# Moving the query weights to ScalarE's queue, and a new order of all work, in an attention and GLU kernel

## The chip, the cores and the metric

The kernel runs on one core of one Trainium2 chip. The time is that of one execution on the device, in microseconds (us). The time before is the median of three runs; one of them was also profiled, and every time inside the kernel comes from that execution. In the profile the engines are called PE (TensorE), PEld (TensorE's weight loads), DVE (VectorE), ACT (ScalarE), POOL (GpSimd) and SP (SyncE). A q behind a name (SPq, ACTq) is the engine's queue, where it issues DMA transfers. Times are counted from the start of the span.

## What is computed

x is 2,048 tokens by 512, in bf16. Two branches read it, and a gate per token mixes them. A is attention with a memory: 32 heads of 16, in four segments of 512 tokens; each segment attends causally to itself, and reads a matrix M and a vector z that collect the keys and values of the segments before. B is a gated GLU with 1,792 inner features.

```python
g = sigmoid((x * gate_w).sum(-1, keepdims=True))
# A: q, k, v = x @ wq, x @ wk, x @ wv, split in heads; per segment s of 512:
a_dot = softmax(q_s @ k_s.T * Dh**-0.5 + causal) @ v_s
a_mem = (phi(q_s) @ M) / (phi(q_s) @ z + 1e-6)
o_s   = sigmoid(beta) * a_mem + (1 - sigmoid(beta)) * a_dot
M, z  = M + phi(k_s).T @ v_s, z + phi(k_s).sum()
a = concat(o_s) @ wo                       # phi(t) = t + 1 if t > 0 else exp(t)
# B:
b = (gelu(x @ w_gate) * (x @ w_up)) @ w_down
return g * a + (1 - g) * b
```

## The kernel before

All weights stay in SBUF once loaded. Tokens go through in four segments (0 to 3), and each segment has the same tasks, named by kind, segment and tile:

- `K`, `Q` (line 448; K of segment 0 is at 476, in three parts a, b, c): projections in four tiles of 128 features, each four matmuls of 512 columns that collect in one PSUM bank. `Kev`, `Qev` (441, 442) evict a bank with ScalarE (`:a`) or VectorE (`:d`). `kpada`, `kpadb` (487) spread the keys for the scores.
- `V` (498) in eight halves of 256 or 257 columns, `Vev` (505, 506). The 257th column is the gate's weight, which `gwtr` and `gwev` (768, 770) put there.
- `st` (601): a fill. Score matmuls of 32 rows, four at a time side by side, fill all four banks of one large PSUM tile (psX). `exp` (608) on ScalarE empties it in one instruction of 2,048 columns; `msk` (614) on GpSimd masks the diagonal. There is one psX, so the next fill waits for this exp. There are 72 fills.
- `pv` (643): probabilities times values, for two tiles at once; `tp`, `pvp`, `ota` (529, 666, 667, 672) on VectorE divide and transpose.
- `G`, `gelu`, `gd`, `U`, `h` (448, 697, 702, 719): the GLU's gate and up tiles, fourteen each; `out` (734) is the down projection, `wo` (748) attention's output projection, `wev` and `oev` (739, 742, 752) mix the two.
- `phk`, `phq` (460 to 464), `ktr`, `mz`, `nd`, `ndp`, `otr`, `otm`: the memory's phi, transposes and products. `vsh` (517) copies values to the other half of the partitions.

Dense results and pv share four PSUM banks; a task that opens a bank names it after a colon in the order (`G0_6:3`).

The order of all work is one list written out, `ORDER`. `schedule` (134) goes through it, takes for each task the engine that the list names, and gives each engine its instructions in the order of the list. Estimates such as `T_MM`, `issue` and `lat` in the tasks don't enter into the program. `plan` and `finalize` (171, 200) put a semaphore wait before each instruction for what it reads or overwrites. Each engine works through its own queue in order, so an instruction that waits holds all behind it, on SyncE and ScalarE their DMA issues too.

Loads are made by `load` and `ld_w` (324, 340). The last argument names another load that must have landed before this one is issued; `ld_x0_t2`, `ld_x0_t3` (361) and `ld_xt` (343) are DMA transposes of x, issued by SyncE. x of segment 0 comes in two ways: tokens 0 to 255 plainly (`x0_0` on SyncE, `x0_1` on ScalarE), turned by eight transposes on TensorE (`xtr0`, 785) and evicted by two copies of 512 columns (`xev0`, 794); tokens 256 to 511 by the two DMA transposes. Two loads of 256 KB bring wk, one on SyncE (blocks 2 and 3 of the contraction), one on ScalarE (blocks 0 and 1). K's part a needs blocks 2 and 3 of the first 256 tokens, part b blocks 0 and 1, part c all four of the last 256 tokens.

Before the data are there, TensorE multiplies ones by ones: `warm1` (45 matmuls of 80 columns) ahead of the transposes, and `warm2` (7 more) behind them (382).

SyncE issues in this order: x0_0, wk1, x0_t2, x0_t3, wq0, wq1, gw, beta, wv (once x0_t3 is there), wg0 (once wq1 is there), the four transposes of x's second segment, wu1, and so on. ScalarE issues x0_1 and wk0 ahead of everything else that it does.

Of the kernel before, what the change touches and what calls it, by code (L numbers as in the profile page):

```python
# [248 lines left out]
def _build(es, nc, A_x, A_wq, A_wk, A_wv, A_wo, A_beta, B_w_gate, B_w_up, B_w_down, gate_w, out):  # L249
# [90 lines left out]
    def ld_w(name, eng, dst, src, writes, size, wait=(), **kw):  # L340
        load(name, eng, lambda e: e.dma_start(dst, src), writes, size=size, wait=[("ld", w) for w in wait], **kw)  # L341
# [39 lines left out]
    for name, n, cols in (("warm1", 45, 80), ("warm2", 7, 80)):  # L381
        one(name, PE, 3.0, [I(lambda e, cols=cols: e.matmul(BK[s0.i][:, 0:cols], ones, ones[:, 0:cols], start=True, stop=True),
                              [], [bk(s0)]) for _ in range(n)], bias=9000.0, opens=name == "warm1")
# [400 lines left out]
    for p in (1, 0):  # L784
        one(f"xtr0_{p}", PE, 4 * T_TR, [I(lambda e, q=q, kb=kb, p=p: e.transpose(
            XB[:, 1024 * p + (kb % 2) * 256 + q * 128:1024 * p + (kb % 2) * 256 + q * 128 + 128],
            pt[stage[0]][:, q, kb * 128:(kb + 1) * 128], ident[:, :]),
            [("xs", 0, 0), ("xs", 0, 1), ("pt", stage[0]), ("ident",)], [("X", p)]) for kb in (2 * p, 2 * p + 1) for q in (0, 1)])
        dst = xT[0][:, 2 * p:2 * p + 2, 0:256]
        xin = XB[:, 1024 * p:1024 * p + 512].rearrange("p (k c) -> p k c", c=256)  # L790
        wr = [("xT", 0, kb, "h0") for kb in (2 * p, 2 * p + 1)]
        task(f"xev0_{p}", [
            (ACT, 0.477, [I(lambda e, dst=dst, xin=xin: e.activation(dst, xin, ACTF.Copy), [("X", p)], wr)]),
            (DVE, 0.335, [I(lambda e, dst=dst, xin=xin: e.tensor_copy(dst, xin), [("X", p)], wr)])], L_DVE)
# [72 lines left out]
exp0_0C Q0_2:0 G0_2:3 V0_2b:2 ld_x1_2 ld_x1_1 betab ld_x1_3 ld_x1_0 st0_0D Vev0_2b:a exp0_0D Gev0_2:d kpadb0_1
Qev0_2:d phka0_0 V1_2b:1 V0_0a:3 G1_6:2 V1_0b:0 Vev1_2b:d phka0_2 st0_0E Vev0_0a:d Vev1_0b:d G0_1:1 bexp Gev1_6:a
exp0_0E Gev0_1:d Q1_2:3 V1_3b:2 V1_3a:0 kpada0_3 Qev1_2:d Vev1_3a:d phkb0_2 phkc0_2 Vev1_3b:d st0_1A gz0 gqa exp0_1A
gr0 Q1_0:1 V1_0a:3 G1_5:0 Vev1_0a:d gqb Gev1_5:d st0_1B Q1_1:2 K1_0:3 exp0_1B phkb0_0 ld_wu1 ld_x2_0 G0_5:0 Qev1_0:d  # L870
kpadb0_3 vsh0_21 st0_1C exp0_1C Qev1_1:d ld_x2_1 ld_x2_3 ktr0_3 ld_wg1 Gev0_5:d V1_2a:1 K1_3:2 K1_1:0 vsh0_01
# [87 lines left out]
```

## Time and profile before

| | us |
|---|---|
| runs | 263.88, 264.18, 264.53 |
| median | 264.18 |
| the profiled execution | 264.53 |
| its span, first to last instruction | 262.8 |
| TensorE busy | 257.9 |
| ScalarE busy | 203.2 |
| VectorE busy | 197.4 |
| GpSimd busy | 99.1 |

The page says that 16.50 MB were moved, and that the granted clock of TensorE was 1.00 of full speed over the whole span. Matmuls overlap in the array, and each is shown from its start to its modelled end, so two neighbours overlap in the record: what a matmul costs is read from the distance of two starts. Busy time in the page is that of the engine having at least one instruction in work. In a line of the timeline stand the start, the length, the engine, the line of the code, the operation, what it writes and reads, its shape, and the count of instructions merged into it; in brackets the idle time ahead of it and what ended it.

### The profile page before, as it was taken

The page shows a single profiled execution, that of the slowest core. Times are in us where ns is not written, and L with a number is a line of the kernel's source. Part 1 is how long each engine was busy: PE and PEld are TensorE (multiplying, and loading weights), DVE is VectorE, ACT ScalarE, POOL GpSimd, SP SyncE. Part 2 cuts the span into 40 slices and gives each one's busy share as a digit, 9 for nine tenths or more (in the row PEclk, how much of TensorE's full clock was granted, in tenths as well). Part 3 has the DMA queues.
Part 4 walks back from the last instruction along what each step waited for, and adds up shares of the span by engine and source line. Part 5 has one row for each costly group of instructions (what it writes and reads, how often), then busy time and mean ns, then how long its engine had stood idle before and what let it go on. Part 6 is the DMA issues. An engine that isn't in the chain of part 4 may idle for free.

```text
span 262.8 us, 6704 instructions
## 1 busy us (share of the span) xinstructions
PE 257.9 (98%) x2849; PEld 122.5 (47%) x2849; DVE 197.4 (75%) x412; ACT 203.2 (77%) x171; POOL 99.1 (38%) x163
## 2 busy tenths in 40 slices
PE   8989999999999999999999999999999999999995
PEld 8645445444454444544445445444444434444542
DVE  1658878284888686778968988976895973899873
ACT  1569879889998878898988898788788788777312
POOL 5006672024500465104806284156500477345300
PEclk9999999999999999999999999999999999999999
DMA  7795699300010211430003100022430000001432
GB/s 186 244 160 144 163 278 275 93 2 1 5 28 2 61 43 39 91 75 2 2 0 71 35 0 2 2 41 61 68 79 0 2 1 22 3 0 42 62 42 80
DMA packets 31974, 16.50 MB, mean 63 GB/s; under 512 B 21576, under 2 KB 31944, under 8 KB 31944
## 3 DMA queue, kind: packets, MB, share of 16 engines
q1 hardware_dynamic: 31528, 15.68, 27.2%
q8 instruction: 22, 0.36, 0.6%
q10 hardware_dynamic: 416, 0.39, 0.4%
q14 instruction: 8, 0.07, 0.1%
HBM read 7.87 MB, written 2.10 MB: 38 GB/s over the span
## 4 chain that ended last, share of the span: by engine, by line
PE 92%; DMA 4%; SPq 1%; issue 0%; DVE 0%; DVEq 0%
PE psD L448 47%; PE psD L734 19%; PE psX L601 9%; PE psD L643 6%; PE psD L748 5%; PE psD L498 5%; DMA wg<-in_B_w_gate_dram 3%; PE psD L546 1%; DMA wq<-in_A_wq_dram 1%; SPq L361 1%; PE psD L576 1%; SPq L341 1%; DVE ost L752 0%; DVEq L817 0%
## 5 line engine op out<-in xcount | busy, mean ns | idle before, releaser
L608 ACT ACTIVATE pt<-psX 128x2048 bf16<-128x2048 f32 x72 | 135.1, 1877 | 29.5 <-PE psX L601 27.9
L614 POOL TENSOR_TENSOR pt<-pt,ctri 128x256 bf16<-128x256 bf16 x128 | 92.6, 734 | 128.3 <-ACT pt L608 123.8
L448 PE MATMUL psD<-xT,wu 128*128 128x512 bf16 x224 | 54.6, 380 | 0.0
L448 PE MATMUL psD<-xT,wg 128*128 128x512 bf16 x224 | 53.4, 380 | 1.1 <-DMA wg<-in_B_w_gate_dram 1.1
L734 PE MATMUL psD<-wd,gb 128*128 128x512 bf16 x224 | 53.2, 380 | 0.0
L719 DVE TENSOR_TENSOR gb<-psD,gb 128x512 bf16<-128x512 f32 x56 | 37.2, 681 | 10.8 <-PE psD L448 10.7
L448 PEld LDWEIGHTS psD<-xT,wg 128*128 128x128 bf16 x224 | 20.8, 98 | 25.8 <-issue 2.6
L734 PEld LDWEIGHTS psD<-wd,gb 128*128 128x128 bf16 x224 | 20.7, 98 | 24.3 <-issue 2.1
L448 PEld LDWEIGHTS psD<-xT,wu 128*128 128x128 bf16 x224 | 20.2, 98 | 24.7 <-issue 2.6
L601 PE MATMUL psX<-qT,kD 32*128 32x192 bf16 (+7 forms) x512 | 28.5, 287 | 0.0
L529 DVE STREAM_TRANSPOSE tT<-psD 128x512 f32<-128x512 f32 x32 | 21.7, 701 | 5.6 <-PE psD L643 5.1
L442 DVE CAST gb<-psD 128x512 bf16<-128x512 f32 x20 | 13.6, 689 | 13.7 <-PE psD L448 13.7
L601 PEld LDWEIGHTS psX<-qT,kD 32*128 32x128 bf16 x512 | 8.2, 92 | 25.1 <-ACT pt L608 13.4
L498 PE MATMUL psD<-wv,xT 128*128 128x257 bf16 (+1 forms) x128 | 18.2, 273 | 0.0
L752 DVE SCALAR_TENSOR_TENSOR ost<-psD,gtok,wds 128x512 bf16<-128x512 f32 (+1 forms) x17 | 11.9, 711 | 7.7 <-PE psD L748 7.6
L667 DVE SCALAR_TENSOR_TENSOR ob<-tT,gq,rc 128x256 bf16<-128x256 f32 x32 | 16.7, 522 | 1.1
L702 ACT ACTIVATE gb<-psD 128x512 bf16<-128x512 f32 x28 | 15.0, 594 | 3.3 <-PE psD L448 3.3
L643 PE MATMUL psD<-pt,vnat 64*17 64x192 bf16 (+7 forms) x512 | 17.1, 283 | 0.0
L643 PE MATMUL psD<-pt,vsh 64*17 64x192 bf16 (+7 forms) x512 | 17.1, 283 | 0.0
L448 PE MATMUL psD<-xT,wq 128*128 128x512 bf16 x64 | 16.3, 379 | 0.0
L748 PE MATMUL psD<-wo,oT 128*128 128x512 bf16 (+1 forms) x68 | 16.2, 367 | 0.0
L498 PEld LDWEIGHTS psD<-wv,xT 128*128 128x128 bf16 x128 | 11.8, 97 | 6.6 <-issue 1.4
(81 smaller groups left out, 257.0 us busy)
## 6 DMA issues: line engine op xcount, KB each, us to landing
out_dram<-ost SPq DMA_DIRECT2D x15, 128.0 KB, 1.8
wg<-in_B_w_gate_dram SPq DMA_DIRECT2D x2, 896.0 KB, 6.5
wu<-in_B_w_up_dram SPq DMA_DIRECT2D x2, 896.0 KB, 8.3
wd<-in_B_w_down_dram SPq DMA_DIRECT2D x2, 896.0 KB, 7.1
vsh<-vnat SPq DMA_DIRECT2D x16, 68.0 KB, 2.9
wq<-in_A_wq_dram SPq DMA_DIRECT2D x2, 256.0 KB, 3.5
wv<-in_A_wv_dram SPq DMA_DIRECT2D x1, 512.0 KB, 4.8
wo<-in_A_wo_dram SPq DMA_DIRECT2D x1, 512.0 KB, 5.0
```

Of the source, the lines that this page charges most:

```text
L448: one(name, PE, n * T_MM, [I(lambda e, i=i: e.matmul(BK[sl.i][:, :], lhs(i), rhs(i), start=(i == 0), stop=(i == n - 1)), reads(i), [bk(sl) ...
L498: one(f"V{s}_{m}{'ab'[hf]}", PE, 2 * T_MM, [I(lambda e, i=i, sl=sl, a=a, z=z, xs=xs: e.matmul(BK[sl.i][:, 0:z - a], xs(i), wv[:, i, a:z], ...
L529: one(f"tp{name}", DVE, 0.605, [I(lambda e, sl=sl, ti=ti: e.transpose(tT[ti][:, :], BK[sl.i][:, :]), [bk(sl)], [("tT", ti)])], bias=bias)
L601: ins.append(I(lambda e, t=t, kb=kb, ncol=ncol, c0=c0, g=g: e.matmul(XALL[:, g * 512 + c0:g * 512 + c0 + ncol], kD[(4 * s + t) % R_KD][32 ...
L608: one(f"exp{s}_{name}", ACT, 2048 * 0.000833 + 0.05, [I(lambda e: e.activation(pt[slot][:, :, :], xin, ACTF.Exp, scale=ATT_SCALE), [("X",) ...
L614: ins.append(I(lambda e, mv=mv: e.tensor_tensor(mv, mv, cm, ALU.mult), [("pt", slot), ("causal",)], [("pt", slot)]))
L643: ins.append(I(lambda e, kb=kb, slot=slot, c0=c0, n=n, g=g, r0=r0, sl=banks[j], va=va: e.matmul(BK[sl.i][32 * g:32 * g + 17, 64 * kb:512], ...
L667: I(lambda e, ti=ti, ri=ri, t=t, j=j, dst=dst: e.scalar_tensor_tensor(out=dst, in0=t_rows(ti), scalar=gq[:, 2 * t + j:2 * t + j + 1], in1= ...
L702: t = one(f"gd{s}_{ft}", ACT, 0.485, [I(lambda e, gi=gi, f=f, sl=sl: e.activation(gb[gi][:, f, :], BK[sl.i][:, :], ACTF.Gelu_apprx_tanh), ...
L719: one(f"h{s}_{ft}", DVE, 0.605, [I(lambda e, sl=sl, gi=gi, f=f: e.tensor_tensor(gb[gi][:, f, :], BK[sl.i][:, :], gb[gi][:, f, :], ALU.mult ...
L734: mm.append(I(lambda e, fb=fb, gi=gi, f=f, q=q, sl=sl: e.matmul(BK[sl.i][:, :], gb[gi][:, f, q], wd[:, fb, :], start=(fb == 0), stop=(fb = ...
L748: one(f"wo{s}_{qt}{sfx}", PE, 4 * T_MM * w / 512, [I(lambda e, kb=kb, q=q, so=so, c=c, w=w: e.matmul(BK[so.i][:, 0:w], oT[:, kb, q], wo[:, ...
```

## The change

Loads of the first microseconds. wk comes in three pieces: block 2 on SyncE, block 3 and then blocks 0 and 1 on ScalarE. wq goes from SyncE's queue to ScalarE's, behind wk. wv waits for the first of the two x transposes, wg0 for wq0, and beta for wq0; in the new order beta is issued behind x's second segment and wg1.

```diff
-    for eng, h in ((SP, 1), (ACT, 0)):
-        ld_w(f"wk{h}", eng, wk[:, halves[h], :], wsrc(A_wk)[:, halves[h], :], [("wk", 2 * h), ("wk", 2 * h + 1)], 0.25)
+    for eng, nm, c in ((SP, "2", slice(2, 3)), (ACT, "3", slice(3, 4)), (ACT, "0", slice(0, 2))):
+        ld_w(f"wk{nm}", eng, wk[:, c, :], wsrc(A_wk)[:, c, :], [("wk", i) for i in range(c.start, c.stop)], 0.125)
...
-    ld_w("wq0", SP, wq[:, halves[0], :], wsrc(A_wq)[:, halves[0], :], [("wq", 0)], 0.25)
-    ld_w("wq1", SP, wq[:, halves[1], :], wsrc(A_wq)[:, halves[1], :], [("wq", 1)], 0.25)
-    ld_w("wv", SP, wv[:, :, 0:512], wsrc(A_wv), [("wv",)], 0.5, ["x0_t3"])
-    ld_w("beta", SP, ball, A_beta.partition_broadcast(P), [("ball",)], 0.02, ["wk0"])
+    ld_w("wq0", ACT, wq[:, halves[0], :], wsrc(A_wq)[:, halves[0], :], [("wq", 0)], 0.25)
+    ld_w("wq1", ACT, wq[:, halves[1], :], wsrc(A_wq)[:, halves[1], :], [("wq", 1)], 0.25)
+    ld_w("wv", SP, wv[:, :, 0:512], wsrc(A_wv), [("wv",)], 0.5, ["x0_t2"])
+    ld_w("beta", SP, ball, A_beta.partition_broadcast(P), [("ball",)], 0.02, ["wq0"])
     ld_xt(1, "wq0")
-    ld_w("wg0", SP, wg[:, :, fhalf[0]], wgr[:, :, fhalf[0]], [("wg", 0)], 0.9, ["wq1"])
+    ld_w("wg0", SP, wg[:, :, fhalf[0]], wgr[:, :, fhalf[0]], [("wg", 0)], 0.9, ["wq0"])
```

The warm-up is one run of 52 matmuls of 66 columns, all ahead of the transposes. The eight transposes are four tasks of two, one for each block, in the order 2, 3, 0, 1, each with an eviction of 256 columns; in the new order ScalarE evicts block 2, VectorE the others.

```diff
-    for name, n, cols in (("warm1", 45, 80), ("warm2", 7, 80)):
...
+    one("warm1", PE, 3.0, [I(lambda e: e.matmul(BK[s0.i][:, 0:66], ones, ones[:, 0:66], start=True, stop=True),
+                             [], [bk(s0)]) for _ in range(52)], bias=9000.0, opens=True)
...
-    for p in (1, 0):
-        one(f"xtr0_{p}", PE, 4 * T_TR, [I(lambda e, q=q, kb=kb, p=p: e.transpose(
...
+    for kb in (2, 3, 0, 1):
+        one(f"xtr0_{kb}", PE, 2 * T_TR, [I(lambda e, q=q, kb=kb: e.transpose(
...
+        dst, xin, wr = xT[0][:, kb, 0:256], XB[:, 1024 * kb:1024 * kb + 256], [("xT", 0, kb, "h0")]
+        task(f"xev0_{kb}", [
+            (ACT, 0.38, [I(lambda e, dst=dst, xin=xin: e.activation(dst, xin, ACTF.Copy), [("X", kb)], wr)]),
+            (DVE, 0.25, [I(lambda e, dst=dst, xin=xin: e.tensor_copy(dst, xin), [("X", kb)], wr)])], L_DVE)
```

All of `ORDER` is new. No task of the kernel is added or dropped but the pieces named above. Its beginning before, and now, and the two later places that the prediction speaks of:

```diff
-ld_x0_0 ld_wk1 ld_x0_1 warm1:0 ident xtr0_1 xev0_1:d xtr0_0 warm2 xev0_0:d vones0 masks ld_wk0 causal1 gwz ld_x0_t2
-ld_x0_t3 ld_wq0 ld_wq1 ld_gw ld_beta causal0 consts K0_1a:1 K0_3a:2 K0_3b K0_2a:3 K0_0a:0 K0_2b K0_0b K0_1b K0_0c
...
+ld_x0_0 gwz warm1:0 ident ld_x0_1 xtr0_2 xtr0_3 causal0 xev0_3:d consts ld_wk3 ld_wk0 ld_wq0 ld_wq1 xtr0_0 xev0_2:a
+xtr0_1 masks causal1 xev0_1:d xev0_0:d ld_wk2 K0_1a:1 ld_x0_t2 ld_x0_t3 ld_gw K0_3a:2 K0_2a:3 K0_0a:0 K0_1b K0_0b
+K0_3b K0_2b K0_1c Kev0_1:d kpadb0_1 vones0 K0_0c K0_3c Kev0_0:a kpada0_0 kpadb0_0 K0_2c Q0_0:1 Q0_2:0 Kev0_3:a
+Kev0_2:d gwtr:2 Qev0_0:a st0_0A exp0_0A Q0_3:3 kpada0_1 gwev ld_wv V0_3b:1 Qev0_2:d Vev0_3b:d V0_2a:2 Vev0_2a:a causal
+phka0_0 V0_1b:0 Vev0_1b:d ld_wg0 ld_x1_0 ld_x1_2 ld_x1_1 ld_x1_3 ld_wg1 ld_beta ld_wu1 st0_0B Qev0_3:a V0_2b:1 V0_3a:2
+V0_0a:3 G0_0:0 exp0_0B kpadb0_3 Vev0_3a:a Vev0_2b:a st0_0C Gev0_0:d kpadb0_2 V0_0b:2 Q0_1:1 G1_6:0 exp0_0C Vev0_0a:a
+Gev1_6:d Qev0_1:d st0_0D G0_5:3 G0_4:0 V1_3a:1 exp0_0D st0_0E Gev0_5:a Vev0_0b:d kpada0_2 Gev0_4:d Vev1_3a:a betab
+G0_6:2 Gev0_6:d G0_1:3 V0_1a:0 vsh0_21 Gev0_1:d Vev0_1a:d ld_x2_1 ld_x2_2 vsh0_00 exp0_0E st0_1A exp0_1A phkb0_0
...
+G1_3:3 Gev1_3:a ld_wd0 out0_1_0:0 out0_1_1 st1_0C out0_1_2 ktr1_0 K2_0:3 Kev2_0:d wev0_1:d G1_13:2 G1_8:1 G1_12:3
+G1_7:0 gelu1 gd1_8 gd1_12 gd1_13 gd1_7 G1_11:1 G1_10:3 gd1_10 G1_9:2 vsh1_21 vsh1_20 ld_x3_1 gd1_11 gd1_9 vsh1_00
+ld_x3_0 phkc1_2 ktr1_2 ld_x3_2 vsh1_01 ld_wo ktr1_1 exp1_0C phqc1_2 pvp0_30 kpadb1_3 ota0_2 ota0_3 mzq0 phqc1_0
...
+msk3_1D pv3_1:0132 exp3_2B st3_2C exp3_2C tp3_d00 U3_5:0 tp3_d01 pvp3_00 U3_10:1 st3_2D ktr2_0 dma9 pvp3_01 h3_5 h3_10
```

wo, which SyncE issued behind wu0 and ahead of all work of segment 1, is now issued in segment 1, behind the DMA transposes ktr1_2, x3_0, x3_1 and x3_2; wg1 is issued ahead of wu1 instead of long behind it.

More of the change, by code (lines that the diff above doesn't have):

```diff
@@ L783, in _build @@
     XB = XALL.bitcast(BF)
[L784 to L786 removed]
+    for kb in (2, 3, 0, 1):
+        one(f"xtr0_{kb}", PE, 2 * T_TR, [I(lambda e, q=q, kb=kb: e.transpose(
+            XB[:, 1024 * kb + q * 128:1024 * kb + q * 128 + 128],
             pt[stage[0]][:, q, kb * 128:(kb + 1) * 128], ident[:, :]),
[L788 to L794, printed above, removed]
+            [("xs", 0, 0), ("xs", 0, 1), ("pt", stage[0]), ("ident",)], [("X", kb)]) for q in (0, 1)])
+        dst, xin, wr = xT[0][:, kb, 0:256], XB[:, 1024 * kb:1024 * kb + 256], [("xT", 0, kb, "h0")]
+        task(f"xev0_{kb}", [
+            (ACT, 0.38, [I(lambda e, dst=dst, xin=xin: e.activation(dst, xin, ACTF.Copy), [("X", kb)], wr)]),
+            (DVE, 0.25, [I(lambda e, dst=dst, xin=xin: e.tensor_copy(dst, xin), [("X", kb)], wr)])], L_DVE)
     head_gates()
@@ L867 @@
[L867 to L871, printed above, removed]
@@ L930 @@
+oev3_2 dma14 wo3_3a:0 wev3_3:a oev3_3b dma15b oev3_3a dma15a
 """
```

118 lines of the change are left out of this document (55 added, 63 removed).

## The prediction

> **What bounds the kernel.** I read the page first, then the waits of TensorE, then its timeline, then the issues of SyncE and ScalarE beside it.
>
> ```profile
> PE 257.9 (98%) x2849; PEld 122.5 (47%) x2849; DVE 197.4 (75%) x412; ACT 203.2 (77%) x171; POOL 99.1 (38%) x163
> ```
>
> TensorE is busy for 98% of the span, so only its idle time and its own work can be saved. Its waits are the start of the program (0.8) and one inside the work, for the gate weights:
>
> ```profile
> PE psD L448 <- DMA wg<-in_B_w_gate_dram: 1.1, 1, 1.1
> ```
> The timeline of TensorE (start, us, count at the end):
>
> ```profile
> 0.82 3.16 PE L382 MATMUL psD<-const-bfloat16-1.0 128*128 128x80 bf16 x45 [0.82 <-PEq L944]
> 3.78 1.05 PE L785 MATMUL psX<-ident,pt 128*128 128x128 bf16 x8
> 4.63 0.65 PE L382 MATMUL psD<-const-bfloat16-1.0 128*128 128x80 bf16 x7
> 5.25 3.65 PE L476 MATMUL psD<-xT,wk 128*128 128x256 bf16 x32
> 8.74 1.89 PE L448 MATMUL psD<-xT,wq 128*128 128x512 bf16 x8
> ...
> 13.54 1.49 PE L498 MATMUL psD<-wv,xT 128*128 128x257 bf16 x12
> 16.12 1.02 PE L448 MATMUL psD<-xT,wg 128*128 128x512 bf16 x4 [1.09 <-DMA wg<-in_B_w_gate_dram]
> ...
> 31.73 1.89 PE L448 MATMUL psD<-xT,wk 128*128 128x512 bf16 x8
> 33.55 0.40 PE L601 MATMUL psX<-qT,kD 32*128 32x320 bf16 x8
> 33.88 1.90 PE L448 MATMUL psD<-xT,wg 128*128 128x512 bf16 x8
> ```
>
> Three readings. The useful work begins at 5.25, and TensorE stands still from 15.03 to 16.12. Starts of neighbours give the true price of work: 0.216 us for a 512-column matmul, 0.109 for 256 columns (32 from 5.25 to 8.74), though one is shown as 0.38 or 0.27 long. So the stand costs 1.09 plus the 0.16 by which a shown end exceeds the next possible start: 1.25 us. And a score fill between dense work costs two changes of tile shape: 33.55-31.73 is 0.09 over 8 x 0.216, and 33.88-33.55 is 0.11 over its 512 columns. From 16.12 to the last wo at 258 the starts leave no other gap above 0.1 us.
>
> Why the gate weights are late is in the issues of SyncE and ScalarE:
>
> ```profile
> 1.71 2.59 SPq L361 DMA_TRANSPOSE xT<-in_A_x_dram  x2
> 4.35 1.09 SPq L341 DMA_DIRECT2D wq<-in_A_wq_dram  x2
> 5.93 0.34 SPq L341 DMA_DIRECT2D omem<-in_gate_w_dram  x1
> 6.31 0.37 SPq L341 DMA_DIRECT2D omem<-in_A_beta_dram  x1
> 6.73 0.42 SPq L341 DMA_DIRECT2D wv<-in_A_wv_dram  x1
> 8.47 0.37 SPq L341 DMA_DIRECT2D wg<-in_B_w_gate_dram  x1
> 8.88 7.11 SPq L345 DMA_TRANSPOSE xT<-in_A_x_dram  x4
> ```
>
> ```profile
> 1.23 0.46 ACTq L341 DMA_DIRECT2D wk<-in_A_wk_dram  x1
> 1.72 1.28 ACT L441 ACT_TABLE_LOAD   x1 [1.72 <-PEq L944]
> ```
>
> wq stands behind two transposes, wg0 waits for wq1 (8.45), and lands 7.5 us later, at 16.0. Between 7 and 9 us the DMA engines are far from full (columns at the end: clock, DMA share, GB/s), with beta, 8 KB in 64-byte pieces that take 3.8 us to land, ahead of wv on the same queue:
>
> ```profile
> 7.00:8.00 1.00, 1.00 (x12) 0.90 (x10) 0.37 (x1) 0.00 (x0) 0.00 (x0) 1.00 0.62 210
> 8.00:9.00 1.00, 1.00 (x11) 0.80 (x9) 1.00 (x3) 0.49 (x1) 0.00 (x0) 1.00 0.26 77
> ```
>
> **The change, part by part.**
>
> *Start of K.* K0's first part needs both key pieces 2 and 3 and the evictions of blocks 2 and 3. ScalarE now issues five transfers, where it issued two, before its table load (L441) and its eviction of block 2. At 0.46 each (its own row; wq on SyncE took 0.55) the fifth ends at 3.1 to 3.4, the table load of 1.28 at 4.35 to 4.65, an eviction of 256 columns (0.39 at L506) at 4.75 to 5.05. The warm-up is 52 x 66 = 3,432 columns against 45 x 80 = 3,600, so the transposes start 0.14 earlier, at 3.65; the VectorE copy of block 3 is done by 4.6 (the first copy came 0.67 after the fourth-last transpose began; half of a 0.425 copy). Pieces of 128 KB land between 2.8 us after issue (x, the same size) and 3.9 (wk, twice the size): 4.05 to 5.15. I take 4.85 for K's start: 0.40 earlier; bounds 4.75 and 5.25.
>
> *Its rate.* Warm-up matmuls stand 0.067 us apart for 80 columns, 0.83 ns a column; K0 runs at 0.43. So the array ran at half rate until about 5.2, though the granted clock reads 1.00 there. From 4.85 to 5.2 half the speed costs 0.15. What remains: 4.85+0.15+3.49 = 8.49 for the first Q, **0.25 gained**. K0's last part needs the second x transpose (landed 6.45) only at 6.7; now wq's 512 KB run beside it, which may cost 0 to 0.5. I take 0, since it begins behind 128 KB less. wq itself is issued at 2.2 and 2.6 instead of 4.35 and 5.0, and lands by 6.8 (3.5 to 4.2 later); Q needs it at 8.49.
>
> *The gate weights.* wv waits for the first x transpose (landed 6.0) and so is issued at 6.0 to 6.4 instead of 6.73; wg0 waits for wq0 (2.15 plus 3.5 to 4.2, so 5.7 to 6.4) and is issued at about 6.7 instead of 8.47. With the 7.5 of its row it lands at 14.2. The new order puts 12 Q matmuls (2.59), 24 V matmuls (2.63), two fills (0.84) and the gate's small one (0.1) between 8.49 and the first gate matmul: 14.65. It lands first, so **1.25 is saved**, with 0.45 to spare; bounds: nothing saved, if it lands at 16.0 as before, and all of it.
>
> *The second x segment* is issued from 6.9 instead of 8.88. Its last transpose landed at 19.5; 2.0 earlier is 17.5. The first use, G1_6, comes at 17.3, and its last block 0.65 later: no wait, up to 0.5 if the transposes are slower. Beta goes behind wg1, to land near 21; VectorE's copies of it (L763) stand at about 21.5, and behind them an eviction that TensorE needs two groups later. Taken as 0.
>
> *The fills of the head.* With the stall gone, ScalarE sets the pace there: between exp0_0A and exp0_0B stand two evictions (0.39 and 0.60), so the exp (1.88) after them ends some 0.15 behind the planned fill; twice such. I take **0.2 lost**, bounds 0 and 0.6.
>
> *The rest of the order.* I counted TensorE's stream in both orders: the same matmuls, 153 changes of tile shape before and 151 after, so 0.2 less. One fill (st3_2D) follows the one before after two U groups only, 2.15 us; the shortest distance that the trace shows is 2.38, so 0.2 is lost. The last 17 us, from pv3_3 on, hold the same groups but for one swap. wo is now issued late: SyncE holds it behind transposes that wait for VectorE's phkc1_2. VectorE's rows after pv0_3 (four transposes of 0.70, four pairs of 0.73, then 3.7) put that at 80.5, wo at 83.7 and, with its 5.0, in place at 88.7; TensorE reaches it at about 89.2. Taken as 0; bound 1.0 lost.
>
> Sum: -0.25 -1.25 +0.2 -0.2 +0.2 = -1.3. The profiled execution took 264.53 (span 262.81 and 1.72 around it) and was the slowest of three; it would become 263.2. Against the median of 264.18 the forecast is **262.9**.
>
> **Rivals.**
>
> *The bytes set the pace.* x, wk, wq, wv and wg0 are 2.94 MB, moved from 1.8 to 16.0, 207 GB/s on the mean, whoever issues them. If that mean stays, wg0 lands at 16.0, the first gate matmul waits 1.35, and all gain before it is eaten: 264.2. For it: DMA shares of 0.8 to 1.3 from 2 to 7 us. Against it: 77 and 210 GB/s at 7 to 9, with 329 right after. The Trainium skill, page "DMA: Bandwidth & Descriptors", section "Issuing engines are not separate DMA queues", says that another issuing engine saves only issue time; by that rule this rival gains weight.
>
> *The array stays at half rate.* After its transposes TensorE now has nothing until K, where seven warm matmuls stood. Full rate came 4.4 us after the first matmul. If the count begins anew at 4.85, it comes at 9.25 and costs 2.2, not 0.15: 262.9+2.05 = 265.0, **slower by 0.3%**. It decides from an opening at about 9.0; from 7.4 on the gain is gone. Against it: the pause is only 0.3 us, and after the stand of 1.09 us at 15.03 the matmuls again start 0.216 apart. The Trainium skill, page "TensorE: Matmul & The Clock Gate", Parts 1 and 4, states a free-running window of some 3.4 us and that transposes don't count as activity. The trace agrees with its two rates (0.83 and 0.43 ns a column). An estimate from that page: the next opening after 5.2 would be 8.6, which would give 264.6.
>
> *ScalarE's queue becomes the gate.* Issues of SyncE's four transposes took up to 2.2 us when transfers stood ahead. If ScalarE's three added issues take that, its table load ends at 9.5 and K starts near 10: 267.7. It is slower from a K start at about 7. Against it: no plain issue in the trace took over 0.63.
>
> *The new order waits elsewhere*: wo, the x transposes, fills behind ScalarE, 0.5 to 2 us in all: 263.4 to 264.9, or a little more.
>
> **Chances.** The measurement tells 0.3%, 0.79 us, from no change: the bounds are 263.39 and 264.97. Forecast 0.45; better still (no head wait, K at 4.75) 0.08; bytes 0.20; waits elsewhere 0.12, of it 0.04 slower; half rate 0.10, half of it slower; ScalarE's queue 0.05. Faster 0.53, same 0.33, slower 0.14. The range is 262.2 (all terms at their good ends) to 265.0, which leaves out the worst of the last three cases.
>
> **What would show it.** K0 starting near 4.85 behind ScalarE's eviction; the first Q near 8.5; no wait of TensorE for wg, with wg0 issued near 6.7; 256-column starts 0.109 apart from 5.2 on; no gap of TensorE near 17, 89 and st3_2D. The prediction is wrong if wg0 is still waited for, if K0's starts are 0.21 apart beyond 5.5, or if gaps above 0.3 us appear after 20 us.

## The result, and the profile after

The kernel after takes **265.76 us** (median of 6 runs, 265.36 to 266.39), the kernel before 264.06 beside it (6 runs, 263.44 to 264.53): a ratio of 1.0063, 95% interval 1.0048 to 1.0077. The change costs 1.7 us. The forecast was 262.9, and 265.76 lies above the range. The profiled execution took 266.39, with a span of 264.65 against 262.81; it was the slowest of its six runs in both kernels.

The waits of TensorE in the kernel after (line numbers from about 350 on differ from those of before: K of the first segment is now L475, the dense products L447, V L497):

```profile
PE psD L475 <- DMA xT<-in_A_x_dram: 1.7, 1, 1.7
PE psD L447 <- issue: 1.1, 7, 0.2
PE psD L475 <- DMA wk<-in_A_wk_dram: 0.9, 1, 0.9
PE psD L381 <- PEq L941: 0.8, 1, 0.8
PE psX L600 <- ACT pt L607: 0.4, 2, 0.3
```

The wait for the gate weights is gone. In its place stand two waits of the K product, for the x transposes and for the key weights. The row with "issue" is no wait: 34 of 2849 matmuls have no record in this trace, and a missing one looks like a gap. Of the others, 0.4 is two fills that wait for ScalarE's exp. The timeline of TensorE in the kernel after:

```profile
0.83 3.02 PE L381 MATMUL psD<-const-bfloat16-1.0 128*128 128x66 bf16 x52 [0.83 <-PEq L941]
3.66 1.04 PE L784 MATMUL psX<-ident,pt 128*128 128x128 bf16 x8
4.97 1.14 PE L475 MATMUL psD<-xT,wk 128*128 128x256 bf16 x8 [0.28 <-ACT xT L790]
7.04 1.03 PE L475 MATMUL psD<-xT,wk 128*128 128x256 bf16 x8 [0.92 <-DMA wk<-in_A_wk_dram]
9.81 1.91 PE L475 MATMUL psD<-xT,wk 128*128 128x256 bf16 x16 [1.73 <-DMA xT<-in_A_x_dram]
11.77 1.68 PE L447 MATMUL psD<-xT,wq 128*128 128x512 bf16 x7
...
16.32 1.49 PE L497 MATMUL psD<-wv,xT 128*128 128x257 bf16 x12
17.64 1.02 PE L447 MATMUL psD<-xT,wg 128*128 128x512 bf16 x3
```

K, one run of 32 matmuls from 5.25 before, now comes in three parts with two stands between them. Its last 16 cost 16 x 0.109 = 1.74 from 9.81, so the first Q is at 11.55 (its record is missing; 11.77 is the second of eight). Before, it was at 8.74. Three numbers then give the whole difference of the two spans:

| | before | after | difference |
|---|---|---|---|
| first Q matmul | 8.74 | 11.55 | +2.81 |
| stand for the gate weights | 1.25 | 0 | -1.25 |
| from the first Q to the end, without that stand | 252.82 | 253.10 | +0.28 |
| span | 262.81 | 264.65 | +1.84 |

The issues behind it, of SyncE and of ScalarE, in the kernel after:

```profile
1.70 2.60 SPq L361 DMA_TRANSPOSE xT<-in_A_x_dram  x2
4.34 0.52 SPq L341 DMA_DIRECT2D omem<-in_gate_w_dram  x1
8.47 0.42 SPq L341 DMA_DIRECT2D wv<-in_A_wv_dram  x1
8.94 0.50 SPq L341 DMA_DIRECT2D wg<-in_B_w_gate_dram  x1
```

```profile
1.23 0.94 ACTq L341 DMA_DIRECT2D wk<-in_A_wk_dram  x2
2.20 1.01 ACTq L341 DMA_DIRECT2D wq<-in_A_wq_dram  x2
3.24 1.28 ACT L790 ACT_TABLE_LOAD   x1 [3.24 <-issue]
4.53 0.38 ACT L790 ACTIVATE xT<-psX 128x256 bf16<-128x256 bf16 x1
```

The two x transposes are issued when they were before, at 1.70, but their time from issue to landing has grown. This is the last line of the view of L361, first of the kernel after, then of the kernel before:

```profile
DMA to landing us min/median/max: 6.6/6.7/6.8
```

```profile
DMA to landing us min/median/max: 3.4/3.8/4.3
```

In landing times: the transposes at 8.46 and 9.67 (before 5.98 and 6.45), the key weights' blocks 0 and 1 at 6.91 (before 5.44), the query weights at 8.31 and 9.32. In the engines' busy time in stretches of 1 us, here of the kernel after, the end of each line has the clock, the busy share of the DMA engines (packets that overlap can bring it above 1) and GB/s:

```profile
5.00:6.00 1.00, 1.00 (x8) 0.76 (x8) 0.23 (x2) 0.00 (x0) 0.00 (x0) 1.00 1.01 105
6.00:7.00 1.00, 0.12 (x2) 0.00 (x0) 0.00 (x0) 0.00 (x0) 0.00 (x0) 1.00 1.18 278
7.00:8.00 1.00, 0.96 (x8) 0.71 (x8) 0.00 (x0) 0.00 (x0) 0.00 (x0) 1.00 1.09 282
8.00:9.00 1.00, 0.07 (x1) 0.00 (x0) 0.00 (x0) 0.00 (x0) 0.00 (x0) 1.00 1.11 135
```

The DMA engines are busy from 5 to 9 while TensorE (first busy column) stands through most of 6 to 7 and of 8 to 9. What they move there is largely the query weights (512 packets of 1 KB, beside 867 of 256 bytes for the transposes), which TensorE can't use before K is done.

### The profile page after: what moved, and what is told of

Its sections match the earlier page's. It is cut to its first block, busy times and chain, and to the rows that moved or that the text cites. A ratio compares the mean times of both kernels' runs of the same rounds, so it can differ in the third digit from the quotient of the medians.

```text
span 264.6 us, 6678 instructions
## 1 busy us (share of the span) xinstructions
PE 254.2 (96%) x2815; PEld 121.6 (46%) x2849; DVE 199.5 (75%) x410; ACT 203.7 (77%) x175; POOL 96.3 (36%) x163
## 3 DMA queue, kind: packets, MB, share of 16 engines
q10 hardware_dynamic: 1104, 1.05, 1.7%
## 4 chain that ended last, share of the span: by engine, by line
PE 91%; DMA 3%; issue 2%; ACT 1%; DVE 1%; SPq 1%; DVEq 0%
PE psD L447 45%; PE psD L733 19%; PE psX L600 9%; PE psD L497 6%; PE psD L747 5%; PE psD L642 5%; DMA xT<-in_A_x_dram 3%; ACT pt L607 1%; PE psD L545 1%; DVE tT L528 1%; PE psD L575 1%; PE psD L475 1%; SPq L361 0%; SPq L341 0%; DVE ost L751 0%
## 5 line engine op out<-in xcount | busy, mean ns | idle before, releaser
L613 POOL TENSOR_TENSOR pt<-pt,ctri 128x256 bf16<-128x256 bf16 x128 | 89.8, 710 | 113.5 <-ACT pt L607 109.0
L447 PE MATMUL psD<-xT,wu 128*128 128x512 bf16 x214 | 53.3, 380 | 0.7 <-issue 0.3
L447 PE MATMUL psD<-xT,wg 128*128 128x512 bf16 x213 | 51.1, 380 | 1.0 <-issue 0.3
L447 PEld LDWEIGHTS psD<-xT,wg 128*128 128x128 bf16 x224 | 20.9, 98 | 24.7 <-issue 1.9
L447 PEld LDWEIGHTS psD<-xT,wu 128*128 128x128 bf16 x224 | 20.4, 98 | 25.2 <-issue 2.8
L441 DVE CAST gb<-psD 128x512 bf16<-128x512 f32 x19 | 12.9, 688 | 8.3 <-PE psD L447 8.0
L666 DVE SCALAR_TENSOR_TENSOR ob<-tT,gq,rc 128x256 bf16<-128x256 f32 x32 | 17.8, 556 | 1.1
L497 PE MATMUL psD<-wv,xT 128*128 128x257 bf16 (+1 forms) x128 | 18.0, 273 | 0.0
L447 PE MATMUL psD<-xT,wq 128*128 128x512 bf16 x61 | 15.5, 380 | 0.3 <-issue 0.2
L497 PEld LDWEIGHTS psD<-wv,xT 128*128 128x128 bf16 x128 | 11.6, 97 | 6.4 <-issue 0.6
L441 DVE CAST kT<-psD 128x512 bf16<-128x512 f32 x12 | 8.2, 687 | 8.3 <-PE psD L475 5.2
## 6 DMA issues: line engine op xcount, KB each, us to landing
wq<-in_A_wq_dram ACTq DMA_DIRECT2D x2, 256.0 KB, 6.4
```

The lines of the kernel that those rows point to most:

```text
L441: (DVE, 0.60, [I(lambda e: e.tensor_copy(dst, src()), [bk(sl), *reads], writes)]),
L447: one(name, PE, n * T_MM, [I(lambda e, i=i: e.matmul(BK[sl.i][:, :], lhs(i), rhs(i), start=(i == 0), stop=(i == n - 1)), reads(i), [bk(sl) ...
L497: one(f"V{s}_{m}{'ab'[hf]}", PE, 2 * T_MM, [I(lambda e, i=i, sl=sl, a=a, z=z, xs=xs: e.matmul(BK[sl.i][:, 0:z - a], xs(i), wv[:, i, a:z], ...
L613: ins.append(I(lambda e, mv=mv: e.tensor_tensor(mv, mv, cm, ALU.mult), [("pt", slot), ("causal",)], [("pt", slot)]))
L666: I(lambda e, ti=ti, ri=ri, t=t, j=j, dst=dst: e.scalar_tensor_tensor(out=dst, in0=t_rows(ti), scalar=gq[:, 2 * t + j:2 * t + j + 1], in1= ...
```

## The experiments

Theories, as the expectations name them. **B**: the 512 KB of query weights are served ahead of what K needs, whichever queue they are on. **A**: it is the second queue; plain loads on ScalarE's queue and transposes on SyncE's hold each other up. **C**: the key weights in three pieces, and their order, make K late. Kernels of one group ran on the same chip.

### First group: where the query weights stand

**e1_wq_sync**: the kernel after, the query weights back behind the transposes on SyncE (in ORDER too).

```diff
-    ld_w("wq0", ACT, wq[:, halves[0], :], wsrc(A_wq)[:, halves[0], :], [("wq", 0)], 0.25)
-    ld_w("wq1", ACT, wq[:, halves[1], :], wsrc(A_wq)[:, halves[1], :], [("wq", 1)], 0.25)
+    ld_w("wq0", SP, wq[:, halves[0], :], wsrc(A_wq)[:, halves[0], :], [("wq", 0)], 0.25)
+    ld_w("wq1", SP, wq[:, halves[1], :], wsrc(A_wq)[:, halves[1], :], [("wq", 1)], 0.25)
```

> The changed kernel with the two wq loads back on SyncE's queue, behind the two x transposes; all else as changed. In the changed kernel blocks 0 and 1 of wk landed at 6.91 and the second x transpose at 9.67 (before: 5.44 and 6.45), and K stood still for 0.92 and 1.73 us. Theory A (two queues: plain loads on ScalarE's queue and DMA transposes on SyncE's hold each other up while both run): the second transpose lands near 6.5, wk near 5.5, K begins near 4.97 and runs through, first Q near 8.5, no wait for wg: 262.3 to 262.9 us. Theory B (bytes: 512 KB of wq are served ahead of what K needs, on whichever queue): the same here, since wq is behind. Theory C (the pieces of wk: blocks 0 and 1, third in ScalarE's queue, are late because of that order): wk still lands near 6.9 and K still stands for about 0.9: 263.6 or more.

263.60 us, ratio to before 0.9973 (0.9951 to 0.9994). Its timeline of TensorE:

```profile
4.54 1.16 PE L475 MATMUL psD<-xT,wk 128*128 128x256 bf16 x8
6.04 2.78 PE L475 MATMUL psD<-xT,wk 128*128 128x256 bf16 x24 [0.34 <-DMA wk<-in_A_wk_dram]
8.66 1.89 PE L447 MATMUL psD<-xT,wq 128*128 128x512 bf16 x8
...
14.75 1.02 PE L447 MATMUL psD<-xT,wg 128*128 128x512 bf16 x4
```

The transposes land at 6.27 and 6.77 (5.98 and 6.45 before), the long stand is gone, and so is the stand for the gate weights. K waits 0.34 for blocks 0 and 1 of the key weights, which landed at 5.91. The landings and the first Q are close to those of A and B; the time, at C's bound of 263.6, is 0.7 above their 262.9. So the loss lies in the place of the query weights, and the rest of the change doesn't cause it.

**e2_before_wq_act**: the kernel before, with only this part of the change.

```diff
-    ld_w("wq0", SP, wq[:, halves[0], :], wsrc(A_wq)[:, halves[0], :], [("wq", 0)], 0.25)
-    ld_w("wq1", SP, wq[:, halves[1], :], wsrc(A_wq)[:, halves[1], :], [("wq", 1)], 0.25)
+    ld_w("wq0", ACT, wq[:, halves[0], :], wsrc(A_wq)[:, halves[0], :], [("wq", 0)], 0.25)
+    ld_w("wq1", ACT, wq[:, halves[1], :], wsrc(A_wq)[:, halves[1], :], [("wq", 1)], 0.25)
```

> The kernel before, with only the engine of the two wq loads changed to ScalarE, behind its half of wk; order, pieces of wk and all else as before. A: the second x transpose lands at 9 or later instead of 6.45, K's last part waits 2 to 3 us, wg0 is waited for less or not at all, so 265 to 266 us. B: a delay by the time of 512 KB at 280 to 330 GB/s, 1.6 to 1.9 us, so the transpose near 8.2 and 264 to 265. C: nothing changes in K, 263.5 to 264.2.

265.18 us, ratio 1.0036 (1.0019 to 1.0053). The timeline of TensorE:

```profile
5.12 2.61 PE L476 MATMUL psD<-xT,wk 128*128 128x256 bf16 x16
8.82 1.91 PE L476 MATMUL psD<-xT,wk 128*128 128x256 bf16 x16 [1.09 <-DMA xT<-in_A_x_dram]
10.57 1.89 PE L448 MATMUL psD<-xT,wq 128*128 128x512 bf16 x8
```

The same wait, made by this edit alone: the last transpose lands at 8.69 instead of 6.45, between the cases of B (8.2) and A (9 or later), and the first Q is 1.83 later.

**e3_wq_sync_first**: the kernel after, the query weights on SyncE as in e1, but issued ahead of the transposes.

```diff
-    ld_w("wq0", ACT, wq[:, halves[0], :], wsrc(A_wq)[:, halves[0], :], [("wq", 0)], 0.25)
+    ld_w("wq0", SP, wq[:, halves[0], :], wsrc(A_wq)[:, halves[0], :], [("wq", 0)], 0.25)
...
-xtr0_1 masks causal1 xev0_1:d xev0_0:d ld_wk2 K0_1a:1 ld_x0_t2 ld_x0_t3 ld_gw K0_3a:2 K0_2a:3 K0_0a:0 K0_1b K0_0b
+xtr0_1 masks causal1 xev0_1:d xev0_0:d ld_wk2 ld_wq0 ld_wq1 K0_1a:1 ld_x0_t2 ld_x0_t3 ld_gw K0_3a:2 K0_2a:3 K0_0a:0 K0_1b K0_0b
```

> The changed kernel with the two wq loads on SyncE's queue ahead of the two x transposes: the bytes come as early as in the changed kernel, but in one queue with the transposes, so that they don't run beside each other. A: the transposes start later, and then run at their own pace (before, some 1.4 us of data for both), second one landing near 8 to 8.5, wk near 5.5 to 6.5; 264 to 264.7 us. B: second transpose near 9.5 as in the changed kernel; 265.5 to 266.

265.4 us in one run. The waits are shifted, and the first Q, at 10.54, stands where e2 has it:

```profile
7.61 1.03 PE L475 MATMUL psD<-xT,wk 128*128 128x256 bf16 x8 [1.18 <-DMA wk<-in_A_wk_dram]
8.80 1.91 PE L475 MATMUL psD<-xT,wk 128*128 128x256 bf16 x16 [0.16 <-DMA xT<-in_A_x_dram]
10.54 1.89 PE L447 MATMUL psD<-xT,wq 128*128 128x512 bf16 x8
```

Ahead in the same queue, the query weights delay the last transpose to 8.67, 1.90 later than in e1. 512 KB in 1.90 us are 276 GB/s, the rate from 6 to 8 above. Their own issue is 0.99 later too (2.70 instead of 1.71), behind the issues of the query weights; but DMA shares are 0.87 to 1.01 from 3 to 6, and no packet of the transposes moves before 5.77 (4.08 in e1), which speaks for the bytes ahead and not for the issue. The landing is nearer to A's 8 to 8.5 than to B's 9.5, the time nearer to B's 265.5. So a second queue isn't needed for a loss of nearly 2 us: it is enough that the query weights are served before K's data.

**e4_wq_act_late**: the kernel after, the query weights on ScalarE, but issued only when the last transpose has landed.

```diff
-    ld_w("wq0", ACT, wq[:, halves[0], :], wsrc(A_wq)[:, halves[0], :], [("wq", 0)], 0.25)
-    ld_w("wq1", ACT, wq[:, halves[1], :], wsrc(A_wq)[:, halves[1], :], [("wq", 1)], 0.25)
+    ld_w("wq0", ACT, wq[:, halves[0], :], wsrc(A_wq)[:, halves[0], :], [("wq", 0)], 0.25, ["x0_t3"])
+    ld_w("wq1", ACT, wq[:, halves[1], :], wsrc(A_wq)[:, halves[1], :], [("wq", 1)], 0.25, ["x0_t3"])
```

> The changed kernel with the two wq loads on ScalarE's queue, behind its first eviction, and only issued once the second x transpose has landed. A: the transposes land near 6.5 and wk near 5.5, K runs through to 8.5; wq is issued near 6.5 and lands near 10 to 10.7, so Q waits for 1.5 to 2 us: 264 to 264.8. C: wk still late, near 6.9.

267.36 us in one run:

```profile
4.54 3.90 PE L475 MATMUL psD<-xT,wk 128*128 128x256 bf16 x32
10.88 3.41 PE L447 MATMUL psD<-xT,wq 128*128 128x512 bf16 x8 [2.45 <-DMA wq<-in_A_wq_dram]
```

K now runs through, with the transposes at 5.96 and 6.39. But the query weights, issued at 6.41 behind the value weights (5.97), land at 10.75 and 11.44, and Q pays more than K gained; the 264 to 264.8 of the expectation are missed by 2.6. It pays twice: after the stand the starts of Q are 0.427 us apart where they are 0.216 elsewhere.

### Second group: dose, pieces, beta

**e5_before_beta**: the kernel before, beta's load issued behind the first gate weight.

```diff
-ld_x0_t3 ld_wq0 ld_wq1 ld_gw ld_beta causal0 consts K0_1a:1 K0_3a:2 K0_3b K0_2a:3 K0_0a:0 K0_2b K0_0b K0_1b K0_0c
+ld_x0_t3 ld_wq0 ld_wq1 ld_gw causal0 consts K0_1a:1 K0_3a:2 K0_3b K0_2a:3 K0_0a:0 K0_2b K0_0b K0_1b K0_0c
...
-Kev0_1:d gwev Q0_3:0 ld_wv ld_wg0 Qev0_1:d V0_1b:1 V0_3a:2 V0_3b:3 exp0_0A Qev0_3:d Vev0_3a:a Vev0_1b:a st0_0B
+Kev0_1:d gwev Q0_3:0 ld_wv ld_wg0 ld_beta Qev0_1:d V0_1b:1 V0_3a:2 V0_3b:3 exp0_0A Qev0_3:d Vev0_3a:a Vev0_1b:a st0_0B
```

> The kernel before with one step alone: beta's load issued behind the first gate weight instead of ahead of the value weights. Theory M (the one of the prediction): the 1.25 us that the first gate matmul waited for its weight in the kernel before came of the late issue behind beta and the first x; the value weights and the gate weight issue up to 1 us earlier, and the wait shrinks by about that: 263.2. Rival N: beta's load costs nothing, since the issue waits for a semaphore of the transposes, not for beta: the wait stays 1.25 and the time at 264.2.

263.95 us, ratio 0.9991 (0.9970 to 1.0012). In the profile the mechanism of M is there:

```profile
9.01 1.89 PE L448 MATMUL psD<-xT,wq 128*128 128x512 bf16 x8
...
13.80 1.49 PE L498 MATMUL psD<-wv,xT 128*128 128x257 bf16 x12
15.37 1.02 PE L448 MATMUL psD<-xT,wg 128*128 128x512 bf16 x4
```

12 V matmuls from 13.80 end the queue at 15.11, so the stand is 0.26 instead of 1.25. The value weights landed at 10.68 instead of 11.52, the gate weight at 15.24 instead of 15.98. But K began 0.27 later, behind key weights that landed later than before though nothing ahead of them was changed, and the times can't tell the gain from none: inconclusive in time.

**e6_wq1_sync**: the kernel after, the second half of the query weights back on SyncE behind the transposes.

```diff
-    ld_w("wq1", ACT, wq[:, halves[1], :], wsrc(A_wq)[:, halves[1], :], [("wq", 1)], 0.25)
+    ld_w("wq1", SP, wq[:, halves[1], :], wsrc(A_wq)[:, halves[1], :], [("wq", 1)], 0.25)
```

> The kernel after with the second half of the query weights back on SyncE behind the x transposes, so that 256 KB instead of 512 KB lie ahead of them. Theory B (bytes served ahead of what K needs): the last x transpose lands near 8.0 instead of 9.67, K's last part starts there, the first query matmul is at about 10.2, and the time is about half-way, 264.6. Theory A (two queues hold each other up while both are filled): the same direction, but the landing goes with how long the ScalarE queue is filled, so 7 to 8. Theory C (the pieces of the key weights make it late): no change of the landing, 265.8.

265.44 us: B's dose failed. 256 KB ahead delay the last transpose to 8.70, not 8.0, as much as all 512 KB ahead in one queue (e3), and the first Q is at 10.58. From e1's 6.77 that is 1.93, where 256 KB at 276 GB/s are 0.95. Something costs more than the bytes, then. In the stretches of e6 (GB/s at the end) the rate is lower at a full share:

```profile
6.00:7.00 1.00, 0.40 (x5) 0.14 (x3) 0.00 (x0) 0.00 (x0) 0.00 (x0) 1.00 1.19 195
7.00:8.00 1.00, 0.91 (x8) 0.57 (x6) 0.00 (x0) 0.00 (x0) 0.00 (x0) 1.00 1.17 184
```

This alone doesn't show that the queues hold each other up: by themselves the transposes move at 156 GB/s with a share of 1.21 (e1, 5 to 6). The packets, below, say where the time went.

**e7_wk_halves**: the kernel after, the key weights in two halves as before, the query weights on ScalarE.

```diff
-    for eng, nm, c in ((SP, "2", slice(2, 3)), (ACT, "3", slice(3, 4)), (ACT, "0", slice(0, 2))):
+    for eng, nm, c in ((SP, "1", slice(2, 4)), (ACT, "0", slice(0, 2))):
```

> The kernel after with the key weights in two halves as in the kernel before, the query weights still on ScalarE. Theory C: the key weights' first blocks land at 5.3 instead of 6.91, the last x transpose at 8.7 instead of 9.67, first query matmul at 10.5, 264.6, as in the kernel before with only the query weights moved. Theories A and B: the bytes ahead are the same, so the landing of the last transpose stays near 9.7 and the time at 265.8.

266.05 us. The key weights land at 5.27 as C has it, but the last transpose still at 9.28, so K only waits longer in its last part: first Q at 11.15. C falls.

**e8_after_again**: the kernel after, unchanged.

> The kernel after, unchanged, profiled once more. If the landings of its first profile are a property of the kernel, the key weights' first blocks land at 6.9 and the last x transpose at 9.7 again, within 0.3. If they are a matter of chance between the two queues, they differ by 1 us or more, and the last 1 us of the loss has no cause in the order of the loads.

266.2 us; key weights 6.90, last transpose 9.47, first Q 11.35. Its landings repeat.

### Third and fourth group: what is left of the loss

The last transpose of the kernel after lands 0.8 to 1.0 later than that of e2. **e9_gw_late**, the kernel after with the gate's small load held back, and **e10_before_wq_act_gw**, e2 with that load early:

```diff
-    ld_w("gw", SP, gw4, gate_w.rearrange("(kb p) -> kb p", p=P), [("gw4",), ("gwz",)], 0.01)
+    ld_w("gw", SP, gw4, gate_w.rearrange("(kb p) -> kb p", p=P), [("gw4",), ("gwz",)], 0.01, ["x0_t2"])
```

```diff
-ld_x0_0 ld_wk1 ld_x0_1 warm1:0 ident xtr0_1 xev0_1:d xtr0_0 warm2 xev0_0:d vones0 masks ld_wk0 causal1 gwz ld_x0_t2
+ld_x0_0 gwz ld_wk1 ld_x0_1 warm1:0 ident xtr0_1 xev0_1:d xtr0_0 warm2 xev0_0:d vones0 masks ld_wk0 causal1 ld_x0_t2
```

> The kernel after, with the small load of the gate's weights (1 KB, behind the x transposes on SyncE's queue) held until the first x transpose has landed. It is what still differs between the kernel before with the query weights on ScalarE (last x transpose landed 8.69, small load issued at 5.92) and the kernel after with the key weights in halves (9.28, issued at 4.36). Theory G: the small load, issued early, slows the transposes ahead of it; now the last transpose lands at 8.7 to 8.9 and the first query matmul is at about 10.6: 265.2. Rival, bytes and chance alone: it lands at 9.3 to 9.7 as in the two profiles of the kernel after, first query matmul 11.3 to 11.8: 266.

> The mirror of it: the kernel before with the query weights on ScalarE, and the gate's small load issued early, at about 4.4 instead of 5.92. Theory G: the last x transpose lands at 9.2 to 9.6 instead of 8.69 and the time is 265.8. Rival: 8.7 again, 265.2. Should it land elsewhere in both, the rest of the loss is scatter between the two queues.

265.93 us with the last transpose at 9.21, between the two cases, and 264.96 with it at 8.49, against G's 9.2. G falls.

**e13_before_wq_act_deps** (e10 with the later loads' waits of the kernel after, and beta behind the gate weight) and **e14_before_head** (e7 with the warm-up, the TensorE transposes and the evictions of the kernel before):

```diff
-    ld_w("wv", SP, wv[:, :, 0:512], wsrc(A_wv), [("wv",)], 0.5, ["x0_t3"])
+    ld_w("wv", SP, wv[:, :, 0:512], wsrc(A_wv), [("wv",)], 0.5, ["x0_t2"])
...
-    ld_w("wg0", SP, wg[:, :, fhalf[0]], wgr[:, :, fhalf[0]], [("wg", 0)], 0.9, ["wq1"])
+    ld_w("wg0", SP, wg[:, :, fhalf[0]], wgr[:, :, fhalf[0]], [("wg", 0)], 0.9, ["wq0"])
```

```diff
-    for kb in (2, 3, 0, 1):
-        one(f"xtr0_{kb}", PE, 2 * T_TR, [I(lambda e, q=q, kb=kb: e.transpose(
...
+    for p in (1, 0):
+        one(f"xtr0_{p}", PE, 4 * T_TR, [I(lambda e, q=q, kb=kb, p=p: e.transpose(
...
```

> The kernel before with the query weights on ScalarE, the gate's small load early, and now also the waits of the kernel after on the later loads (value weights behind the first x transpose, gate weight behind the first half of the query weights, beta behind the gate weight). Two cases in which this kernel's transposes landed early (8.5 and 8.7) stand against four of the kernel after (9.2 to 9.7). If the later loads make the difference, the last x transpose now lands at 9.2 or later and the time is 265.8; if the head's own work does (warm-up, transposes on TensorE, evictions), it lands at 8.5 to 8.7 and the time is 265.0.

> The kernel after with the key weights in halves and, in addition, the head of the kernel before: warm-up in two stretches, TensorE's own x transposes in two groups, both evicted by VectorE. If the head's own work makes the difference, the last x transpose lands at 8.5 to 8.7, the first query matmul is at 10.5, 265.2; if the later loads do, it lands at 9.2 or later, 266. If this and the other both land early or both late, the rest of the loss is scatter of the transfers and has no place in the code.

265.3 us (last transpose 8.81) and 265.82 (9.09). Neither half moves it: both lie between the two groups that they were to tell apart. No line of the code that these runs tried makes this part of the loss.

### A version that keeps the gain

**e11_wk_four**: e1 with the key weights in four pieces, two on each queue. **e12_wq_sync_again**: e1 once more.

```diff
-    for eng, nm, c in ((SP, "2", slice(2, 3)), (ACT, "3", slice(3, 4)), (ACT, "0", slice(0, 2))):
+    for eng, nm, c in ((SP, "2", slice(2, 3)), (ACT, "3", slice(3, 4)), (SP, "1", slice(1, 2)), (ACT, "0", slice(0, 1))):
```

> The version of the kernel after with the query weights back behind the x transposes on SyncE, and the key weights in four pieces: blocks 2 and 1 on SyncE ahead of the transposes, blocks 3 and 0 on ScalarE. If what is left at the head is the order of the bytes, the 0.34 that K waits for its first blocks goes, the transposes land at most 0.5 later (needed at about 6.9, landed at 6.8 so far), first query matmul at 8.4: 263.3. Rival: one more issue ahead of the transposes on SyncE delays them by 0.5, K waits there instead, 263.6 to 264.

> The kernel after with the query weights back behind the x transposes on SyncE, measured again beside the kernel before in five rounds. If it is the order of the rest that makes it faster than both kernels (no wait for the gate weight), it is at 263.6, a ratio of 0.9975 with an interval that leaves out 1; if the first measurement was luck, 1.000.

264.07 us, ratio 1.0000 (0.9986 to 1.0014), and 264.04 us, ratio 0.9994 (0.9985 to 1.0003). In e11 the wait for the key weights went, and a smaller one for the transposes came, as its rival said, though not for its reason: they landed at 6.71, no later than e1's 6.77, but K was there sooner:

```profile
4.53 2.14 PE L475 MATMUL psD<-xT,wk 128*128 128x256 bf16 x16
6.85 1.91 PE L475 MATMUL psD<-xT,wk 128*128 128x256 bf16 x16 [0.18 <-DMA xT<-in_A_x_dram]
8.59 1.89 PE L447 MATMUL psD<-xT,wq 128*128 128x512 bf16 x8
```

e12 lost 0.76 to half rate at K's start, and 0.2 to the gate weights, which landed at 15.01 where e1 has them at 14.10. Each against the kernel before beside it, e1 is 1.8 to 2.4 us faster than the kernel after; it beats the kernel before in one group by 0.3%, in the other not measurably: no version here is shown to be faster than the kernel before.

### The landings side by side

| kernel | ScalarE's last load landed | last x transpose landed | first Q | us |
|---|---|---|---|---|
| before | 5.44 | 6.45 | 8.74 | 264.06 |
| e1 / e12 | 5.91 / 5.64 | 6.77 / 6.53 | 8.66 / 8.85 | 263.60 / 264.04 |
| e6, one half ahead | 8.10 | 8.70 | 10.58 | 265.44 |
| e10 / e2 / e13 | 8.10 / 8.17 / 8.42 | 8.49 / 8.69 / 8.81 | 10.37 / 10.57 / 10.68 | 264.96 / 265.18 / 265.3 |
| e14 / e9 / e7 | 8.60 / 8.85 / 8.78 | 9.09 / 9.21 / 9.28 | 10.97 / 11.09 / 11.15 | 265.82 / 265.93 / 266.05 |
| e8 / after (the same kernel) | 9.12 / 9.32 | 9.47 / 9.67 | 11.35 / 11.55 | 266.2 / 265.76 |

Times without an interval above are of one run (after: of six and one). From the last landing to the first Q, third column to fourth, it is 1.9 in all but the kernel before and e12, where K itself was later than its data: K's last part starts 0.14 after the landing and takes 1.74. And in every kernel with query weights on ScalarE ahead, the transposes end 0.35 to 0.60 behind the last load of that queue. The packets of one kernel fit that: from 6 to 8 us in the kernel after, 449 packets of 1 KB (query weights) and 392 of 256 bytes (transposes) were moved. Packet by packet the plain loads take four fifths of the bytes, and the transposes, 1,024 packets, come out last. The Trainium skill, page "DMA: Bandwidth & Descriptors", section "Queues, rings and completion order", says that each DMA engine takes turns between the queues it has work for, a packet at a time. The row just given agrees in this stretch, though not in every stretch of every run (516 to 85 from 7 to 8 in e10).

The packets also tell the two parts of the loss apart. At the usual length of a packet (0.046 us for 1 KB, 0.018 for 256 bytes) and spread over 16 engines, an estimate of the work up to the transposes' last packet is 3.4 to 3.6 us with the query weights behind them (before, e1, e4, e5, e11, e12), 4.25 in e6 and 4.9 in the nine profiles with 512 KB ahead: 0.8 for 256 KB and 1.4 for 512, in step with the bytes as B has it. What it took, from the first packet to that one, is longer by 0.6 to 0.8 in the first group, by 1.1 to 1.4 in e2, e3, e10 and e13, and by 1.8 to 2.3 in e6, e7, e8, e9, e14 and the kernel after. That is packets that took longer than usual, many of them 0.5 to 1.2 us, ending together. So e6's missing 1 us, and the 0.8 to 1.0 between e2 and the kernel after, are such packets and not bytes. What makes them isn't shown. It is not a second queue for the query weights alone, as e3 has 1.4 of it without one.

## Why the prediction was wrong

*The failed step* is in "Its rate": the query weights' "512 KB run beside it, which may cost 0 to 0.5. I take 0, since it begins behind 128 KB less". It measured 3.2 at the last transpose (6.45 to 9.67), and the first Q came 2.81 later instead of 0.25 earlier: 3.06 of the 3.1 by which the sum, -1.3, misses +1.84. Two things were overlooked. The bytes were counted for the gate weights alone (the rival "the bytes set the pace") and not for K, although K's last data had only 0.25 us to spare, 6.45 against 6.7, and 512 KB at the rates of two busy stretches of the kernel before (331 and 276 GB/s) are 1.6 to 1.9 us:

```profile
4.00:5.00 1.00, 1.00 (x14) 1.00 (x13) 0.55 (x2) 0.00 (x0) 1.00 (x3) 1.00 1.20 331
6.00:7.00 1.00, 1.00 (x12) 0.89 (x11) 0.00 (x0) 0.00 (x0) 0.00 (x0) 1.00 0.82 276
```

And issue order was taken as order of service, though the two queues are served side by side. e3 shows the first as a cost of 1.9, e2 the whole as 2.2 at the landing. By the estimate from the packets, 1.4 of the 3.2 is the bytes, and 1.8 is packets that took longer than usual; nothing in the prediction allowed for these, and their cause stays open.

*Start of K*: said 4.85, measured 4.97, behind ScalarE's eviction as said. *Rate*: K's starts are 0.109 apart from 5.30 on, said 5.2. The estimate from the Trainium skill, page "TensorE: Matmul & The Clock Gate", Parts 1 and 4, an opening at 8.6, isn't borne out by that; the rival of the half rate did not come true in the kernel after (e12 shows its milder form, 0.76).

*The key weights* were assumed in time; the second K part waited 0.92 for them. In this kernel that wait costs nothing of its own, since e7 removes it and the last part waits longer.

*The gate weights*: wg0 was issued at 8.94, not 6.7, as its wait for the first half of the query weights (landed 8.31, not 6.4) and the value weights' wait for the transpose moved with the failed step. The 1.25 are saved all the same: it landed at 14.84, 5.9 after issue, and is needed at 17.64. By e1 (landed 14.10, needed at 14.75) the saving doesn't need the late Q. But its margin is small: the same load took 5.9 us from issue to landing in the kernel after and 7.3 in e8, the same kernel, and in e12, the kernel of e1, it landed at 15.01 and 0.2 of the stand was back. So the saving was right, at 1.05 to 1.25, and with a first Q as early as forecast it is partly luck whether all of it comes.

*The order of the rest*: said +0.2 in all (fills 0.2, shape changes -0.2, st3_2D 0.2). From first Q to the end, without a stand for the gate weights, it is 253.10 to 253.13 in ten profiles with the new order (e4, at half rate there, left out) and 252.8 to 252.9 in five with the old: +0.2 to +0.3. The parts weren't measured apart. wo, beta and the second x segment made no wait.

*ScalarE's queue as the gate*: its two loads of query weights took 1.01 to issue, 0.5 each, and the table load began at 3.24. Right to leave out, though "no plain issue in the trace took over 0.63" misses one of 0.71 (SyncE, 23.26). *The bytes*: the rival's 2.94 MB are 2,944 KB, so 3.01 MB and 212 GB/s; nothing hangs on it.

*The end of the range* failed with its cost: 0 to 0.5 should have been 0 to 1.9 by the two stretches above, which puts the high end near 266. *Profile and median*: both profiled executions were the slowest of six, 0.5 (before) and 0.6 (after) above the median, so some of the 1.25 may be smaller in most runs. It is argued, not shown; it would fit that e5 and e12 gain less in time than in their profiles.

## What to carry to other kernels

Before a load is moved ahead, ask what the full DMA engines would have served in that time, and who needs it first: bytes that aren't needed yet push back those that are, and a second issuing engine doesn't hide them. The least price is bytes over the rate of a busy stretch (here 512 KB, 1.6 to 1.9 us), less the slack of the transfer pushed back (here 0.25). It can be more: here 512 KB on the other queue cost 2.0 to 3.2 at the landing, and 256 KB as much as 1.9. In these kernels the place for the next stage's weights was behind the DMA transposes in the same queue; held back until these had landed, and issued behind the value weights (e4), they came too late.
